# A list scheduler's landing times and its tables, in a kernel of landmark attention, routed experts and a gated unit

## The chip, the cores and the metric

The kernel runs on one core of a Trainium2 chip. The metric is the device time of one execution in microseconds (us). The core has a matrix engine (TensorE, PE in the profile, with PEld for its weight loads), VectorE (DVE), ScalarE (ACT), GpSimd (POOL) and SyncE (SP), which issues DMA transfers. Each engine takes its instructions in the order in which they were written for it; between engines semaphores set the order.

## The reference

```python
def _attn_ref(q, k, v):                  # 4 batches, 8 heads, 576 tokens, 64 wide
    m = 32                               # landmarks: means over 18 tokens each
    q_lm = q.reshape(B, H, m, S // m, D).mean(axis=3)
    k_lm = k.reshape(B, H, m, S // m, D).mean(axis=3)
    A = sm(q, k_lm)                      # sm: scaled scores, softmax by rows
    Bm = sm(q_lm, k_lm)
    C = sm(q_lm, k)
    Z = Bm.T / (norm1(Bm) * norm_inf(Bm) + 1e-06)
    for _ in range(6):
        Z = 2 * Z - Z @ Bm @ Z
    return A @ Z @ C @ v

def _moe_ref(x, w_gate, w1, w2, capacity):   # 2304 tokens, 512 wide, 8 experts
    logits = x @ w_gate
    expert = argmax(logits)              # one expert for each token
    gate = softmax(logits)[expert]
    # the first `capacity` tokens of an expert, in order:
    #   out = gate * (relu(x @ w1[expert]) @ w2[expert]); the others give 0

def reference(...):
    x = attn_out as 2304 x 512           # heads side by side
    x = _moe_ref(x, ...)
    return (sigmoid(x @ w_gate) * (x @ w_val)) @ w_out      # 1536 wide inside
```

All arrays are float32.

## The kernel before

**Blocks.** The 2304 tokens are four batches ("blocks" 0 to 3) of 576. Attention is computed for all four blocks. The experts' work is done per pair of a block and an expert: two such pairs are begun early, under the names "lead" and "1", with the attention of later blocks in between, and a list of the pairs that hold tokens is made once all blocks' routing is known; with these inputs three pairs are active (the third is "2"). The final gated unit follows for each pair. A float32 product on PE is done as products of a high part (`hi`) and a low part (`lo`) of each operand; ACT casts the high part, DVE or POOL subtracts it from the whole to get the low part.

**Stages of a block b.** `load_qk` loads q and k (each as 2 x 2 tiles of 128 x 576). `sums` makes the landmarks, on DVE by one reduction of 128 x 576 per tile, or on POOL, for the (b, q or k) listed in `SUMS`, by five additions for a pair of tiles. `inverse` makes `Bm` (product `pb`) and the six steps of Z: in each, PE makes `pz`, ACT copies it (`rz<-pz`), PE and DVE make the next `rz` from it (`rz<-rz,pz`). A step is thus a chain over three engines, and what PE has between two `pz` covers it. `scores` makes `A` (product `pa`, tile `ea`); `weights` is its softmax: `ma` (maximum, DVE), `ea<-ea,ma` (subtraction, on the engine `SUBS[b]`), exponential (ACT), `ra` (sum and reciprocal, DVE), `ea<-ea,ra` (division, on `NORMS[b]`), transposes into `at` (DVE). `context` makes `C @ v` (`pc`, `pct`, `pv`), `back` folds (`pf`), and routes: `pw`, `pgt`, its copy `lt` on ACT, `pg`, then `dl`, `eq`, `mns` (the chosen expert) on DVE.

**Gate, rows, list.** `gate(b)` takes the exponential `gexp` (ACT), its sum `sgm` and reciprocal (DVE), stores the gates to memory (L1756) and for blocks 0 and 1 loads them back spread over all partitions (`gate_now`, L1760). `parts` and `halves` split `at` of block b into `hi` and `lo`; for blocks 2 and 3 `hi` is a tile `xs` of which there is one only (`xs<-at`, two casts on ACT), so block 3's casts wait until block 2's `xs` has been stored. `lo` is `at<-at,xs`, on the engine `XLO[b]`. `row_store` stores `hi`, `lo` and the fold to memory (L1787, L1787, L1791). `ranks` waits for `mns` of all four blocks: DVE makes `ranks` and `rsum`, PE counts in `pk` and `pr`, and the list follows (`pp`, `prow`, `ptb`). `zero_rows` stores zeros to the output in 18 pieces (L1177).

**Expert weights.** `expert_loads` loads an expert's weights in pieces `w_raw` (L613); a piece of the first matrix is multiplied by a fold (`mm<-w_raw,fold`), one of the second is split into `ws` by ACT's cast and DVE's subtraction. The products with them are `mm<-xa,ws`, `mm<-xb,ws` and `mm<-slot,ws`.

**What sets the order.** All of this is written as streams: Python generators that yield what the next step needs (an engine, slots, events). `Streams.go` takes, among the steps that can begin, the one with the earliest modelled start plus `SLACK` times its urgency (`URGENCY` by stage, `EXTRA` by stage and block), and writes it. `Streams.settle` books the time of what was written: a duration for each operation, and for a DMA a landing time from a rate (`RATE`), after which its event counts as done (`SETTLED` later). So a wrong booking costs nothing by itself; it sets in which place of an engine's in-order queue an operation stands. `HOLD` ties loads and stores to an expert load; `WHOLE` makes `context` wait for all of its tiles; `Streams.fill_up` puts products without use (`idle`) where PE would have little to do. All engines' operations are recorded at one line, L114, by the helper `Clocked`.

Of the kernel before, what the change touches and what calls it, by code (L numbers as in the profile page):

```python
# [23 lines left out]


URGENCY = dict(
    load=200,
    sums=150,
    inverse=0,
    scores=0,  # L30
    context=10,
    back=10,
    weights=30,
    ranks=5,
    number=-20,
    lead_rows=10,
    rows=40,
    lead_loads=-50,
    lead_split=0,
    fold=20,  # L40
    lead=20,
    narrow=40,
)
STEP = 2
AHEAD = 0
SUMS = ()
LOWS = "dve"
XLO = ("pool", "pool", "dve", "dve")
SUBS = ("dve", "dve", "pool", "dve")
NORMS = ("pool", "pool", "pool", "pool")  # L50
SQUARES = ("dve", "dve", "dve", "dve")
HOLD = (15, -1, 3, -1)
EXTRA = dict(back3=-15, context3=-30, inverse3=-60, lead_loads2=-100, lead_loads3=200, lead_rows0=60, lead_rows1=60, lead_split1=30, lead_split2=-60, load3=-30, rows1=60, scores1=-15, sums1=-30, weights2=30)
SLACK = 0.003
SWITCH = (0.09, 0.13)
STICK = 0.02
WHOLE = (1, 0, 1, 1)


def free_size(*aps):  # L60
# [22 lines left out]
def pointers(args):  # L83
    return sum(hasattr(a, "shape") for a in args[2:])


COSTS = {
    "pe": pe_cost,
    "dve": lambda op, args: (0.07 + (0.007 if op == "reciprocal" else 1.04e-3) * free_size(*args)
        + 0.06 * (op == "tensor_scalar" and pointers(args) > 0), 0),  # L90
    "act": lambda op, args: (0.052 + 0.83e-3 * free_size(*args) + 0.09 * (op != "copy" and pointers(args)), 0),
    "pool": lambda op, args: (0.3 + 1.42e-3 * free_size(*args), 0),
}
# [25 lines left out]
class Streams:  # L119
# [8 lines left out]
    LAG = 0.2  # L128
    SHARED = 0.5
    SETTLED = 0.3  # L130
    SAME = 0.13

    WINDOW = 3.4133
    THRESH = 2800
    MARGIN = 1.2
    SOON = 0.0
    SPAN = 3.4
    LANES = 8
    RATE = 0.36
    SHORTEST = 96  # L140

    def __init__(self, nc, slots):
        self.log = []
        for name, engine in zip(COSTS, (nc.tensor, nc.vector, nc.scalar, nc.gpsimd)):
            setattr(self, name, Clocked(name, engine, self.log))
        self.free = dict.fromkeys((*COSTS, "sp"), 2.0)
        self.slots = {kind: [0.0] * n for kind, n in slots.items()}
        self.events = {}
        self.live = []
        self.moving = 0.0  # L150
        self.landed = [0.0] * self.LANES
        self.busy = {}
        self.recent = []
        self.urgency = 0
        self.engine = None
        self.fill = None
# [81 lines left out]
    def settle(self, at, engine):  # L238
        first = True
        for what, name, value, columns in self.log:  # L240
            if what == "run":
                if first:
                    first = False
                elif name != engine:
                    at += self.LAG
                elif name != "pe":
                    at += self.SAME
                at = max(at, self.free[name])
                if name == "pe":

                    warm = self.warm(at)
                    value *= 1 if warm else 2
                    for window in range(int(at / self.WINDOW), int((at + value) / self.WINDOW) + 1):
                        share = min(at + value, (window + 1) * self.WINDOW) - max(at, window * self.WINDOW)
                        self.busy[window] = self.busy.get(window, 0) + columns * share / max(value, 1e-9)
                    self.recent.append((at, columns))
                if name == "pool":

                    self.free["dve"] = max(self.free["dve"], at) + self.SHARED * value
                at += value  # L260
                self.free[name], engine = at, name
            elif what == "move":
                if not first and engine != "sp":
                    at += self.LAG
                first, engine = False, "sp"
                at = max(at, self.free["sp"]) + 0.47
                self.moving = max(at + 1.0, self.moving) + value * 1e-6 / self.RATE
                self.landed = [*self.landed[1:], self.moving + 0.64]
                for event in name:
                    self.events[event] = self.landed[-1] + self.SETTLED  # L270
                self.free["sp"] = max(at, self.landed[0])
            elif what == "free":
                self.slots[name].append(at + self.LAG)
            elif what == "done":
                self.events[name] = at + value + self.LAG
            else:
                self.live.append([(at, engine), value, *self.resume(name, value), name])
        self.log.clear()
        return at, engine
# [43 lines left out]
def tile_attention_moe_glu(  # L323
# [15 lines left out]
    B, S, D = v.shape  # L339
# [116 lines left out]
    lead_rows = (("lead", xa, fold_now, idx_lead), ("1", xb, fold_one, idx_one))  # L456
# [236 lines left out]
    w_raw = {}  # L693
# [79 lines left out]
    works, temps, rows = [], [], []  # L773
# [426 lines left out]
    with actx:  # L1200
# [13 lines left out]
        for t in wrs:  # L1214
# [4 lines left out]
        run = Streams(  # L1219
            nc, dict(bank=7, raw=3, cv=2, qk=6, s3=1, ea=2, ec=2, xs=1, sg=2, w=4, ws0=1, ws1=1, ws2=1, ws3=1)  # L1220
        )
        use(run)
        pe, dve, act, pool = run.pe, run.dve, run.act, run.pool
# [13 lines left out]
        def load_qk(b):  # L1237
            for w, src in enumerate((q, k)):
                for g in range(G):
                    if b < 2:  # L1240
                        t = slot(4 * b + 2 * w + g, F32)
                    else:
                        held = [f"w_raw_lead{HOLD[b]}"] if HOLD[b] >= 0 else []
                        yield "sp", "qk", *held
# [32 lines left out]
        def sums(b, w, g, src):  # L1277
            ld = lds[b % 2]
            free = [f"{what}{b - 2}" for what in ("scores", "context", "inverse")]
            if (b, w) in SUMS:  # L1280
                yield "pool", "s3", *[f"raw{b}{w}{g}{kk}" for kk in range(2)], *free
# [146 lines left out]
        def weights(b, u, ea):  # L1428
# [5 lines left out]
            dve.tensor_reduce(ma, ef, AX.X, ALU.max)  # L1434
            yield (SUBS[b],)
            getattr(run, SUBS[b]).tensor_tensor(ef, ef, ma.unsqueeze(2).broadcast_to(shape), ALU.subtract)
            yield ("act",)
# [7 lines left out]
            dve.reciprocal(ra, ra)  # L1445
            yield (NORMS[b],)
            getattr(run, NORMS[b]).tensor_tensor(ef, ef, ra.unsqueeze(2).broadcast_to(shape), ALU.mult)
            for g in range(G):
# [295 lines left out]
        def gate(b, dl):  # L1744
            yield ("act",)
            ge = wk.tile([P, J, E], F32, tag="gexp", name=f"gexp{b}")
            act.activation(ge, dl, AF.Exp)
            yield ("dve",)
            sg = wk.tile([P, J], F32, tag="sgm", name=f"sgm{b}")
            dve.tensor_reduce(sg, ge, AX.X, ALU.add)  # L1750
            yield ("dve",)
            dve.tensor_scalar_add(sg, sg, 1e-9)
            yield ("dve",)
            dve.reciprocal(gates[:, b], sg)
            yield ("sp",)
            nc.sync.dma_start(gate_dram[b], gates[:, b])  # L1756
            run.moved(4 * S, f"gate{b}")
            if b < LEADS:
                yield "sp", f"gate{b}", *[f"y_lead{d}{half}" for d in range(KD) for half in range(2) if b]
                nc.sync.dma_start(gate_now, gate_dram[b].rearrange("p j -> (p j)").partition_broadcast(128))  # L1760
                run.moved(4 * 128 * S, f"gate_{lead_rows[b][0]}")

        def parts(b, u):

# [6 lines left out]
            act.copy(hi, at[:, :, u])  # L1771
            yield (XLO[b],)
            getattr(run, XLO[b]).tensor_tensor(lo, at[:, :, u], hi.bitcast(F32), ALU.subtract)
            run.done(f"scaled{b}{u}")
# [8 lines left out]
        def row_store(b):  # L1783
            held = [f"w_raw_{lead_rows[b][0]}{HOLD[b]}"] if b < LEADS and HOLD[b] >= 0 else []
            yield "sp", f"scaled{b}0", f"scaled{b}1", f"fold{b}0", f"fold{b}1", *held
            for i, part in enumerate(halves(b)):
                nc.sync.dma_start(  # L1787
                    x_dram[b].rearrange("p (a g u t) -> p a g u t", a=2, g=G, u=2)[:, i], part.bitcast(F32)
                )
                run.moved(4 * 128 * G * T)  # L1790
            nc.sync.dma_start(fold_dram[b].rearrange("p (k m) -> p k m", m=LM), st[b]["fold"])  # L1791
            run.moved(4 * 128 * H // 2 * LM, f"x{b}")
            if b >= LEADS:
                run.release("xs")
            run.done(f"rows{b}")

        def block_list():

# [112 lines left out]
    with tc.For_i(1, n_blocks, 1) as i, tc.manual_schedule(engines=ENGINES):  # L1911
        run = Streams(
            nc, dict(bank=3, sg=2, raw=3, w=4, **{f"ws{k}": 1 for k in range(6)},
                **{f"acc{c}": 1 for c in range(TC)}, **{f"slot{k}": 1 for k in range(4)}, work=10, temp=6)
        )
# [70 lines left out]
```

## Time and profile before

| | us |
|---|---|
| median of 3 runs | 551.8 |
| the runs | 554.17, 550.1, 551.8 |
| profiled execution, its time | 550.84 |
| its span in the profile | 549.1 |
| PE busy | 525.6 |
| mean granted clock of PE, as a share of the full one | 0.99 |

A row of a timeline gives the start and the length of a stretch of one kind of operation, engine, line, operation, output and inputs, shapes and count; in brackets the idle time of its engine before it and what ended that. Where many operations overlap, as on PE, starts and ends of neighbours do too. Times are from the start of the span. The clock column of a stretch is the mean granted clock of PE, where 1.00 is the full one.

### The profile page before, as it was taken

How to read it: one execution, taken by the hardware profiler on the slowest of the kernel's cores; microseconds unless marked ns; L12 is line 12 of the kernel's file. 1: busy time of each engine (PE TensorE's matmuls, PEld its weight loads, DVE VectorE, ACT ScalarE, POOL GpSimd, SP SyncE). 2: the span in 40 equal slices, each digit the busy share in tenths (PEclk: the TensorE clock that was granted, in tenths of full speed). 3: DMA queues.
4: the chain of work that ended last, by engine and by line, in shares of the span. 5: the costliest groups of instructions: out<-in, count | busy, mean ns of one | idle time of the engine just before them, and what ended most of it. 6: DMA issues, size and time to landing. Idle time of an engine off the chain costs nothing. (4 is left out here: it accounts for less than half of the span.)

```text
span 549.1 us, 12467 instructions
## 1 busy us (share of the span) xinstructions
PE 525.6 (96%) x4744; PEld 469.9 (86%) x4744; DVE 443.5 (81%) x1167; ACT 301.7 (55%) x766; POOL 35.6 (6%) x48
## 2 busy tenths in 40 slices
PE   6899999987999999999999999999999999999993
PEld 2457878767999999999999999988799999999882
DVE  7897899967879999989997999954476899987442
ACT  1454525355278777676456766733353577776231
POOL 1112102020000000000010100000300000000003
PEclk9999899999899999999999999999999999999998
DMA  8638971499354555561060000000630000000002
GB/s 297 223 90 273 367 250 47 141 315 286 132 228 157 191 193 190 168 210 50 2 222 2 30 21 1 1 1 0 196 125 1 1 1 2 1 1 1 1 1 91
DMA packets 33187, 61.89 MB, mean 113 GB/s; under 512 B 3584, under 2 KB 13440, under 8 KB 33120
## 3 DMA queue, kind: packets, MB, share of 16 engines
q1 hardware_dynamic: 32016, 57.48, 31.6%
q0 software_dynamic: 1104, 3.54, 1.9%
q8 instruction: 39, 0.64, 0.5%
q14 instruction: 28, 0.23, 0.1%
HBM read 47.76 MB, written 13.25 MB: 111 GB/s over the span
## 5 line engine op out<-in xcount | busy, mean ns | idle before, releaser
L114 PE MATMUL mm<-xa,ws 128*128 128x288 f32 x918 | 134.6, 298 | 1.0 <-ACT sg L114 0.7
L114 PEld LDWEIGHTS mm<-xa,ws 128*128 128x128 f32 x918 | 127.4, 189 | 4.9 <-ACT sg L114 0.9
L114 PE MATMUL acc<-ws,slot 128*128 128x512 f32 x504 | 125.2, 392 | 0.0
L114 PE MATMUL mm<-slot,ws 128*128 128x288 f32 x816 | 116.9, 297 | 0.0
L114 PEld LDWEIGHTS mm<-slot,ws 128*128 128x128 f32 x816 | 111.4, 189 | 1.8 <-issue 0.5
L114 PEld LDWEIGHTS acc<-ws,slot 128*128 128x128 f32 x504 | 91.3, 188 | 16.6 <-issue 0.6
L114 PE MATMUL mm<-xb,ws 128*128 128x288 f32 x636 | 96.5, 297 | 0.0
L114 PEld LDWEIGHTS mm<-xb,ws 128*128 128x128 f32 x636 | 89.4, 189 | 2.9 <-PE pgt L114 0.5
L114 DVE TENSOR_TENSOR work<-mm,work 128x288 f32<-128x288 f32 x66 | 30.0, 454 | 10.8 <-PE mm L114 8.5
L114 ACT CAST slot<-work 128x288 fp32r<-128x288 f32 x56 | 22.0, 431 | 29.0 <-PE acc L114 22.1
L114 DVE TENSOR_TENSOR slot<-work,slot 128x288 fp32r<-128x288 f32 (+2 forms) x80 | 26.6, 363 | 13.4 <-ACT slot L114 13.4
L114 ACT COPY work<-mm 128x288 f32<-128x288 f32 x63 | 24.8, 397 | 18.8 <-PE mm L114 11.5
L114 ACT CAST ws<-wg_res 128x256 fp32r<-128x256 f32 (+1 forms) x60 | 26.8, 448 | 13.3 <-PE mm L114 11.3
L114 DVE TENSOR_TENSOR ws<-wg_res,ws 128x256 fp32r<-128x256 f32 (+1 forms) x60 | 28.3, 473 | 2.9 <-ACT ws L114 2.7
L114 ACT CAST ws<-wv_res 128x256 fp32r<-128x256 f32 (+1 forms) x60 | 26.6, 448 | 5.6 <-PE mm L114 4.1
L114 ACT CAST ws<-rows 128x256 fp32r<-128x256 f32 x66 | 26.7, 405 | 5.4 <-DVE rows L114 3.1
L114 DVE TENSOR_TENSOR ws<-wv_res,ws 128x256 fp32r<-128x256 f32 (+1 forms) x60 | 28.2, 473 | 1.0 <-ACT ws L114 0.8
L114 DVE TENSOR_TENSOR ws<-rows,ws 128x256 fp32r<-128x256 f32 x66 | 27.6, 418 | 0.8 <-ACT ws L114 0.8
L114 DVE TENSOR_TENSOR ws<-wo_res,ws 128x512 fp32r<-128x512 f32 x36 | 24.5, 689 | 1.4 <-ACT ws L114 1.0
L114 ACT CAST ws<-wo_res 128x512 fp32r<-128x512 f32 x36 | 21.8, 619 | 6.4 <-DVE wo_res L114 3.5
L114 ACT ACTIVATE slot<-mm 128x288 fp32r<-128x288 f32 x40 | 16.2, 410 | 12.9 <-PE mm L114 12.6
L114 DVE SCALAR_TENSOR_TENSOR slot<-mm,slot 128x288 fp32r<-128x288 f32 x40 | 17.9, 447 | 3.9 <-ACT slot L114 3.6
(243 smaller groups left out, 701.8 us busy)
## 6 DMA issues: line engine op xcount, KB each, us to landing
w_raw<-in_moe_w SPq DMA_DIRECT2D x48, 256.0 KB, 4.1
raw_g<-in_moe_w_gate SPq DMA_DIRECT2D x12, 512.0 KB, 3.8
raw_v<-in_moe_w_val SPq DMA_DIRECT2D x12, 512.0 KB, 3.5
raw_o<-in_moe_w_out SPq DMA_DIRECT2D x12, 512.0 KB, 3.8
out<-zeros SPq DMA_DIRECT2D x18, 256.0 KB, 4.7
vs<-in_v SPq DMA_DIRECT2D x8, 512.0 KB, 5.1
slot<-in_q SPq DMA_DIRECT2D x8, 288.0 KB, 5.8
slot<-in_k SPq DMA_DIRECT2D x8, 288.0 KB, 6.1
```

Of the source, the lines that this page charges most:

```text
L114: return getattr(self.engine, op)(*args, **kwargs)
```

## The change

Two kinds of edit. The bookings: the store of the gates counts as done at a fixed time behind its issue, the load that spreads it is booked at more than twice its size, events of `w_raw` come 1.0 instead of 0.3 behind the modelled landing, the rate of the transfers is 0.39 instead of 0.36, and the tile `xs` is free for block 3 when block 2's row store has landed, no more when it was issued. The tables: urgencies, holds and the engines of four kinds of operation. The stage `sums` of block 3 goes to POOL (`SUMS`), `lo` of blocks 2 and 3 goes from DVE to POOL (`XLO`), the subtraction of blocks 0, 1 and 3 from DVE to POOL (`SUBS`), the division of blocks 0 and 1 from POOL to DVE (`NORMS`). Lines of the changed file stand 1 to 3 below those of before.

```diff
 URGENCY = dict(
-    load=200,
+    load=40,
     sums=150,
     inverse=0,
     scores=0,
-    context=10,
-    back=10,
-    weights=30,
-    ranks=5,
+    context=20,
+    back=0,
+    weights=10,
+    ranks=-200,
     number=-20,
-    lead_rows=10,
-    rows=40,
-    lead_loads=-50,
-    lead_split=0,
-    fold=20,
+    lead_rows=60,
+    rows=10,
+    lead_loads=-100,
+    lead_split=30,
+    fold=10,
     lead=20,
-    narrow=40,
+    narrow=60,
 )
...
-SUMS = ()
+SUMS = ((3, 0), (3, 1),)
...
-XLO = ("pool", "pool", "dve", "dve")
-SUBS = ("dve", "dve", "pool", "dve")
-NORMS = ("pool", "pool", "pool", "pool")
+XLO = ("pool", "pool", "pool", "pool")
+SUBS = ("pool", "pool", "pool", "pool")
+NORMS = ("dve", "dve", "pool", "pool")
 SQUARES = ("dve", "dve", "dve", "dve")
-HOLD = (15, -1, 3, -1)
-EXTRA = dict(back3=-15, context3=-30, inverse3=-60, lead_loads2=-100, lead_loads3=200, lead_rows0=60, lead_rows1=60, lead_split1=30, lead_split2=-60, load3=-30, rows1=60, scores1=-15, sums1=-30, weights2=30)
+HOLD = (11, 3, 11, 15)
+EXTRA = dict(context3=-30, inverse1=-15, inverse3=-60, lead_loads1=100, lead_loads3=-60, lead_rows0=60, lead_rows3=100, load0=100, load1=100, rows0=60, sums0=30, sums1=-60, sums2=-60, weights2=30)
...
-WHOLE = (1, 0, 1, 1)
+WHOLE = (0, 0, 1, 1)
...
     SETTLED = 0.3
+    LATE = 1.0
...
-    SOON = 0.0
+    SOON = 0.6
...
-    RATE = 0.36
+    RATE = 0.39
...
-        self.free = dict.fromkeys((*COSTS, "sp"), 2.0)
+        self.free = dict.fromkeys((*COSTS, "sp"), 2.0) | {"sp": 0.75}
...
                 for event in name:
-                    self.events[event] = self.landed[-1] + self.SETTLED
+                    self.events[event] = self.landed[-1] + (self.LATE if "w_raw" in event else self.SETTLED)
...
             nc.sync.dma_start(gate_dram[b], gates[:, b])
-            run.moved(4 * S, f"gate{b}")
+            run.moved(4 * S)
+            run.done(f"gate{b}", 4.0)
             if b < LEADS:
                 yield "sp", f"gate{b}", *[f"y_lead{d}{half}" for d in range(KD) for half in range(2) if b]
                 nc.sync.dma_start(gate_now, gate_dram[b].rearrange("p j -> (p j)").partition_broadcast(128))
-                run.moved(4 * 128 * S, f"gate_{lead_rows[b][0]}")
+                run.moved(9 * 128 * S, f"gate_{lead_rows[b][0]}")
...
             run.moved(4 * 128 * H // 2 * LM, f"x{b}")
+            run.done(f"rows{b}")
             if b >= LEADS:
+                yield None, f"x{b}"
                 run.release("xs")
-            run.done(f"rows{b}")
```

The order that comes out differs on every engine from the start of the program. Three places show it. Numbers behind a name tell apart tiles of one name; they are drawn anew in each kernel.

DVE at the steps of block 1's inverse, before (`rz` are the steps' results, `ws_69<-w_raw` the split of an expert weight, `slot` a unit's activations, `at` the transposes of block 1):

```order
L114 TENSOR_TENSOR rz_988<-rz_962,pz_979 128x2x32
L114 SCALAR_TENSOR_TENSOR slot_866<-mm,slot_866 128x288
L114 STREAM_TRANSPOSE at_564<-ea_606 128x288
L114 SCALAR_TENSOR_TENSOR slot_991<-mm,slot_991 128x288
L114 TENSOR_TENSOR ws_69<-w_raw,ws_69 128x512
L114 TENSOR_TENSOR rz_1029<-rz_988,pz_1020 128x2x32
```

and after:

```order
L114 TENSOR_TENSOR rz_942<-rz_906,pz_933 128x2x32
L114 TENSOR_TENSOR ws_72<-mm,ws_72 128x512
L114 TENSOR_TENSOR rz_967<-rz_942,pz_958 128x2x32
L114 STREAM_TRANSPOSE at_633<-ea_660 128x288
L114 SCALAR_TENSOR_TENSOR slot_814<-mm,slot_814 128x288
L114 SCALAR_TENSOR_TENSOR slot_850<-mm,slot_850 128x288
L114 TENSOR_TENSOR rz_990<-rz_967,pz_981 128x64
```

The split of the weight that was just loaded (`ws_69<-w_raw`) stood ahead of the last `rz` but one and now comes behind the last, five operations later; ACT's cast for it moved in the same way, behind the last copy `rz<-pz`.

SP ahead of block 2's row store, before (`out<-zeros` are the zero stores, `gate_rows<-gates` the store of block 2's gates):

```order
L1177 DMA out<-zeros 128x4x128 x8
L1756 DMA gate_rows<-gates 96x6
L1177 DMA out<-zeros 128x4x128 x2
L613 ISA
L613 DMA w_raw<-in_moe_w 128x512
L1177 DMA out<-zeros 128x4x128 x2
L1787 DMA x_rows<-xs_2189 128x1152
```

and after (`vs` is block 3's v):

```order
L1267 DMA vs_1809<-in_v 64x512
L1178 DMA out<-zeros 128x4x128 x17
L614 ISA
L614 DMA w_raw<-in_moe_w 128x512
L614 ISA
L614 DMA w_raw<-in_moe_w 128x512
L1178 DMA out<-zeros 128x4x128
L1789 DMA x_rows<-xs_2172 128x1152
```

Seventeen of the zero stores now stand in one row right behind the load of block 3's v, and only two weight loads and one zero store stand between them and block 2's row store; the gates' stores of blocks 2 and 3 come behind it.

POOL from the division of block 2 on, before:

```order
L114 TENSOR_TENSOR ea_1333<-ea_1333,ra_1591 128x576
L114 TENSOR_TENSOR ea_1371<-ea_1371,ra_1615 128x576
L114 MEMSET ranks 96x960
L114 TENSOR_TENSOR ea_1723<-ea_1723,ra_2112 128x576
L114 TENSOR_TENSOR ea_1739<-ea_1739,ra_2149 128x576
```

and after, from the last of the four groups of sums on (`s` is the sums' own tile, `ld` the landmarks, all of block 3):

```order
L114 TENSOR_TENSOR s_1606<-qk_1367 128x384
L114 TENSOR_TENSOR s_1606<-s_1606,qk_1367 128x384
L114 TENSOR_TENSOR s_1606<-s_1606 128x2x96
L114 TENSOR_TENSOR ld_160<-s_1606 128x64
L114 TENSOR_TENSOR ld_160<-ld_160,s_1606 128x64
L114 TENSOR_TENSOR ea_1313<-ea_1313,ra_1685 128x576
L114 TENSOR_TENSOR ea_1328<-ea_1328,ra_1709 128x576
L114 TENSOR_TENSOR ea_1990<-ea_1990,ma_2095 128x576
L114 TENSOR_TENSOR ea_2017<-ea_2017,ma_2098 128x576
L114 MEMSET ranks 96x960
L114 TENSOR_TENSOR at_1312<-at_1312,xs_2172 128x2x288 x2
```

The divisions of block 2 now stand behind the landmarks of block 3, and the subtractions of block 3 and the low parts of block 2 (`at<-at,xs`) are new on POOL.

## Rows read from the trace of the kernel before

**Rows 1.** The page, its first part: busy time of each engine.

```profile
PE 525.6 (96%) x4744; PEld 469.9 (86%) x4744; DVE 443.5 (81%) x1167; ACT 301.7 (55%) x766; POOL 35.6 (6%) x48
```

**Rows 2.** Waits of PE, 42.75 to 150 us: in total, times, longest.

```profile
PE pk L114 <- DVE rsum L114: 2.8, 1, 2.8
...
PE pz L114 <- issue: 0.6, 1, 0.6
```

**Rows 3.** Timeline of PE, 137 to 147 us.

```profile
137.15 0.60 PE L114 MATMUL pk<-ones,rsum 96*32 96x1 f32 x14 [2.79 <-DVE rsum L114]
...
138.42 1.79 PE L114 MATMUL mm<-xb,ws 128*128 128x288 f32 x6
...
140.33 1.70 PE L114 MATMUL mm<-slot,ws 128*128 128x288 f32 x6
```

**Rows 4.** Timeline of PE, 55 to 67 us.

```profile
56.12 0.33 PE L114 MATMUL pz<-rz 32*32 32x32 f32 x16 [1.57 <-DVE rz L114]
56.37 3.22 PE L114 MATMUL mm<-xa,ws 128*128 128x288 f32 x12
...
64.50 1.86 PE L114 MATMUL mm<-xa,ws 128*128 128x288 f32 x12
```

**Rows 5.** Windows: length, PE, PEld, DVE, ACT, POOL busy, clock, DMA share, GB/s.

```profile
56.10:60.00 3.90, 3.88 (x44) 3.54 (x44) 2.24 (x6) 1.80 (x5) 1.42 (x1) 0.56 1.05 367
75.00:95.00 20.00, 19.34 (x280) 16.08 (x265) 19.09 (x53) 8.43 (x28) 4.91 (x4) 1.00 0.37 113
...
137.15:147.10 9.95, 9.95 (x80) 9.34 (x81) 8.76 (x28) 1.96 (x4) 0.00 (x0) 0.83 0.29 97
```

**Rows 6.** Timeline of DVE, 134 to 138 us.

```profile
135.41 0.20 DVE L114 TENSOR_REDUCE sgm<-gexp 96x6 f32<-96x48 f32 x1 [3.02 <-ACT gexp L114]
```

**Rows 7.** Timeline of ACT, 129 to 136 us.

```profile
133.99 1.25 ACT L114 CAST xs<-at 128x576 fp32r<-128x576 f32 x2 [2.90 <-DMA x_rows<-xs]
```

**Rows 8.** Timeline of SP, 108 to 132 us: issue of transfers.

```profile
118.28 6.55 SPq L1177 DMA_DIRECT2D out<-zeros  x8
...
129.21 0.64 SPq L1787 DMA_DIRECT2D x_rows<-xs  x1
```

**Rows 9.** Timeline of ACT, 54 to 57 us.

```profile
54.59 0.62 ACT L114 CAST ws<-w_raw 128x512 fp32r<-128x512 f32 x1 [1.73 <-DMA w_raw<-in_moe_w]
...
55.41 0.20 ACT L114 COPY rz<-pz 128x64 f32<-128x64 f32 x1
```

**Rows 10.** Timeline of PE, 22 to 27 us: steps of block 0's inverse.

```profile
22.47 0.47 PE L114 MATMUL pz<-rz 32*32 32x64 f32 x16 [0.69 <-DVE rz L114]
...
26.05 0.43 PE L114 MATMUL pz<-rz 32*32 32x64 f32 x16 [0.59 <-DVE rz L114]
```

**Rows 11.** Timeline of PE, 96 to 137 us: the products `pgt` of blocks 2, 3.

```profile
119.26 0.68 PE L114 MATMUL pgt<-at,wr 128*32 128x288 f32 x3 [1.04 <-issue]
...
128.97 0.69 PE L114 MATMUL pgt<-at,wr 128*32 128x288 f32 x8
```

**Rows 12.** Groups of DVE by form, 9 to 150 us: busy, mean ns of one.

```profile
L114 DVE TENSOR_REDUCE ld<-qk 128x32 f32<-128x576 f32 x16 | 11.2, 734 | 0.0
...
L114 DVE TENSOR_TENSOR ea<-ea,ma 128x576 f32<-128x576 f32 x6 | 4.5, 753 | 0.1
```

**Rows 13.** Groups of POOL by form, whole span.

```profile
L114 POOL TENSOR_TENSOR ea<-ea,ra 128x576 f32<-128x576 f32 x8 | 9.1, 1158 | 43.3 <-DVE rz L114 35.6 <-DVE ra L114 5.8 <-ACT ws L114 1.9
...
L114 POOL TENSOR_TENSOR xa<-at,xa 128x576 fp32r<-128x576 f32 x2 | 2.8, 1405 | 2.7 <-ACT xa L114 2.7
L114 POOL TENSOR_TENSOR ea<-ea,ma 128x576 f32<-128x576 f32 x2 | 2.6, 1312 | 25.4 <-DVE ma L114 25.4
```

**Rows 14.** Timelines of POOL and DVE, 80 to 94 us.

```profile
85.88 1.16 POOL L114 TENSOR_TENSOR ea<-ea,ma 128x576 f32<-128x576 f32 x1 [3.41 <-DVE ma L114]
...
86.40 1.19 DVE L114 TENSOR_TENSOR ws<-w_raw,ws 128x512 fp32r<-128x512 f32 x1
...
88.63 0.69 DVE L114 TENSOR_TENSOR ws<-w_raw,ws 128x512 fp32r<-128x512 f32 x1
```

## The prediction

> **What bounds the kernel now.** The page's first part comes first: PE is busy for 96% of the span and POOL for 6% [rows 1], so time can come only from PE's gaps, from stretches at the lower clock, and from work taken off PE. The order gives PE 4910 instructions in both kernels, and from its 2356th on the same order, so units "1" and "2" and the tail should take what they take now. What is left is the stretch up to about 150 us, and I read PE's waits in it.
>
> The largest wait is 2.8 us, of `pk` for `rsum` [rows 2]. [...] The chain back: DVE's `sgm` waited 3.02 for ACT's `gexp` [rows 6]; `gexp` stood in ACT's queue behind block 3's two `xs` casts, which waited 2.90 for the landing of block 2's row store [rows 7]; SP had issued that store only at 129.21, behind zero stores, eight of which held it for 6.55 [rows 8]. ACT is in order, so one late landing held the gate and with it the block list.
>
> The second place is the last step of block 1's inverse: `pz` at 56.12 waited 1.57, and the 12 `mm` behind it took 3.22 against 1.86 [rows 4] at a clock of 0.56 [rows 5]. There ACT's cast of an expert weight waited 1.73 for its DMA, with the copy that the step needs behind it [rows 9].
>
> The rest is small: 0.6 and 1.0 with releaser "issue" [rows 2, 11], and in block 0's inverse 0.69 before the first step and 0.59 before a later one [rows 10].
>
> **The change part by part.** The sum goes against the profiled execution, 550.84 (span 549.1 and 1.74 around it).
>
> *Landing of the row store, earlier store.* In the changed order 17 zero stores go in one burst, long ahead, and block 2's store has behind it only two weight loads and one zero store to pass. SP's stretch for the 17 is 17 x 0.82 = 14 us [rows 8]; those loads wait behind it, and nothing shown to PE so far does, since the weights there are for later products. Let T be the start of block 2's `pgt`. Its casts stand close behind the copy of that product: 0.7 + 0.4 + 1.25 + some 0.8 for two short operations between them, so the store is issued by about T + 3.7, and at 4.8 from issue to release (129.21 to 133.99 [rows 7, 8]) it has landed at T + 8.5. Block 3's casts are wanted behind its own `pgt`, which now comes 9.7 after block 2's [rows 11]; the order has 12 `mm` fewer (-1.9) and 32 fold products more (+1.1) between them, and with product and copy this is T + 10. So the casts no longer wait, 1.5 to spare; and 36 `mm` instead of 24 lie ahead of `pk`. That takes 2.8, and with it the lower clock: 1.79 + 1.70 - 1.86 = 1.6. **-4.4**, between -4.4 and 0. What is late next there is DVE's `rsum`, some small operations behind `gexp`; the 12 extra `mm` (1.9) cover them.
>
> *Late expert weights.* ACT and DVE now have the last copy and addition of block 1's inverse ahead of the cast, so a late DMA holds only work that PE wants later: 1.57 + (3.22 - 1.86) = **-2.9**, between -2.9 and 0. Next behind it is the weight itself; before its products stand others, so I book nothing.
>
> *Subtractions of blocks 0, 1 and 3 to POOL, divisions of 0 and 1 to DVE.* A subtraction takes 0.75 on DVE [rows 12] and 1.31 on POOL [rows 13]. In block 0's head two leave DVE's row ahead of `rz`, where PE waited 0.69 [rows 10], and two divisions come back later, between steps. Gain up to 2 x 0.75 = 1.5; loss, where POOL's longer run is waited for, up to 2 x 0.56 = 1.1. Part of the 0.69 is the nearest row: **-0.5**.
>
> *The sums of block 3, and POOL's other work.* POOL gains 20 operations for sums, 6 subtractions and 4 of `lo`, and loses 4 divisions. The sums have no row: by elements against 1158 ns for 576 [rows 13], the five of a group take 0.77 + 0.77 + 0.39 + 0.13 + 0.13 = 2.2, 8.8 for four; at a full operation each, 20 x 1.16 = 23.2. I take 12, nearer to the lower end because the pieces are short. With 6 x 1.31 + 4 x 1.41 - 4 x 1.16 = 8.9 that is 21 us more on POOL. DVE is relieved of 8 reductions at 0.73, and of 4 `lo` and 6 subtractions, and given 4 divisions, all these at the subtraction's 0.75 for the same elements [rows 12]: 5.9 + 3.0 + 4.5 - 3.0 = 10.4. PE waited little for DVE where these stand (20.00 long, 19.34 busy from 75 to 95 [rows 5]), so the relief alone is worth 0 to -0.9.
>
> Against it stands the neighbour: DVE's `ws` took 1.19 while POOL's subtraction ran and 0.69 two us later without it [rows 14]. At 0.5 for each 1.16 of POOL, 21 us could stretch DVE by 9, about what it was relieved of. On PE's path lie only stretched operations ahead of a step of an inverse: 12 steps and DVE operations in blocks 2 and 3 at 0.5 are the upper end, 6; three of them are my value: **+1.5**, between -0.9 and +6.
>
> [...]
>
> *Thinner cover of block 3's inverse.* In the new order five of its steps have only `pct`, `pf` or 8 `pa` between them instead of 6 `mm`. A step with nothing behind it cost PE 0.59 [rows 10]. Five give 3.0, none 0; I take two: **+1.2**.
>
> *Moved without a price.* Idle fillers (14 in both), holds and loads: their work stands in stretches where PE has products in front. The "issue" waits (1.6) fell where zeros were stored; the burst is stored elsewhere, so they may go or come: 0, from -1.6 to +1.6.
>
> Sum: -4.4 - 2.9 - 0.5 + 1.5 + 1.2 = -5.1, so 545.7. The median of the runs shown, 551.8, lies 0.96 above the profiled execution; half of it added gives **546.2**.
>
> **The rivals.**
>
> *Everything is covered* and the small waits go too: no contention on PE's path and no thin steps (-2.7), the issue waits gone (-1.6), is 546.2 - 4.3 = 541.9, with 540.5 to 544 around it. For it: DVE has slack there [rows 5]. Against: short covers showed waits already [rows 10].
>
> *A wait takes the place of the one removed.* Block 3's inverse or the list waits once for 1.5 to 2.8 at another place and the clock falls behind it as it did twice: 546.2 + 2.8 + 1.6 = 550.6, 548.5 to 551.5. For it: both waits of over 1.5 brought the lower clock with them [rows 4, 5].
>
> *The change does not do what it says*: block 3's casts still wait for the landing, as with the burst of zeros still under way at T or a store that lands later than 4.8 behind loads. Then only the second place is gained: 550 to 551.
>
> *Slower: POOL's queue becomes the bound.* POOL is in order, and block 2's divisions are on it behind sums of block 3. At 23.2 for these in place of 12 the last landmark comes 11.2 later and `pb` of block 3 stands still for what of it is not covered. From 5.6 uncovered on the kernel is slower than before; half uncovered gives 551.8, all with one fall of the clock 546.2 + 11.2 + 1.6 = 559, and with the contention of the longer queue (another 3 of its 6) 562. I write 552 to 562. For it: POOL's three kinds of full operation take 1.2 to 1.4 each [rows 13]. Against it: the pieces have two thirds, a third and a ninth of such a one's elements, and POOL is idle for 94% now [rows 1].
>
> **How the numbers follow.** Forecast 0.45, with 544 to 548.5 as its own range; everything covered 0.23; a wait in place of another 0.20; the change not doing what it says 0.03; POOL's queue 0.09. Within 1% of 551.8, about what a measurement of this kernel can tell from no change, is 546.3 to 557.3. Half of the forecast's case and all of the covered one are faster: 0.22 + 0.23 = 0.45. The other half, the two middle cases and the lower half of POOL's are same: 0.23 + 0.20 + 0.03 + 0.04 = 0.50. Slower is POOL's upper half, 0.05. The range runs from 541.5, which leaves out a third of the covered case, to 551.5, which leaves out POOL's: about 0.83.
>
> **What would show it.** In the profile of the changed kernel: no wait of `pk` over 0.5 us and a clock near 1.00 behind it; block 3's first `xs` cast without a DMA as releaser; block 1's last step with under 0.5 of wait; POOL's sums near 12 us in all, and DVE's two-input operations at 1.0 to 1.2 beside them; block 3's `pz` with waits of 0.2 to 0.6. I am wrong if PE's waits before 150 us are as long in sum as now but named by POOL or by `pb`, if the clock falls at a new place, or if the stretch behind 150 us takes another time.

## The result, and the profile after

| | before | after |
|---|---|---|
| median, us (4 runs each) | 550.95 | 543.57 |
| lowest to highest | 549.92 to 554.17 | 542.87 to 545.19 |
| profiled execution, its time | 550.84 | 544.08 |
| its span | 549.1 | 542.2 |

The ratio is 0.986 (95% interval 0.981 to 0.991): 1.4% faster. The forecast was 546.2 (range 541.5 to 551.5).

The page's first part of the changed kernel, against [rows 1]:

```profile
PE 521.8 (96%) x4744; PEld 466.8 (86%) x4744; DVE 443.7 (82%) x1153; ACT 302.7 (56%) x766; POOL 59.0 (11%) x74
```

PE is busy 3.8 us less with the same instructions; the two stretches at the lower clock [rows 4, 5], which are gone, make about 2.5 of it. POOL is busy 23.4 more (21 was forecast). DVE, which by the forecast's count was relieved of 10.4 us of work, is busy for as long as before (443.7 against 443.5): its other operations grew by about as much. PE's waits of the changed kernel from 42 to 150 us and from there on (in total, times, longest):

```profile
PE mm L114 <- DVE slot L114: 0.8, 1, 0.8
PE pn L114 <- DVE bb L114: 0.5, 1, 0.5
PE pk L114 <- DVE rsum L114: 0.4, 1, 0.4
PE pz L114 <- DVE rz L114: 0.2, 1, 0.2
PE pp L114 <- DVE act_b L114: 0.2, 1, 0.2
...
PE mm L114 <- ACT sg L114: 2.4, 1, 2.4
PE acc L114 <- DMA w_raw<-in_moe_w: 1.4, 1, 1.4
```

Against [rows 2]: `pk` waits 0.4 in place of 2.8, no "issue" wait is left, and what else PE waits for are four small waits on DVE, those for `slot` and `bb` new. The last two lines stand behind 150 us. The timeline of PE in the changed kernel, 10 to 150 us, against [rows 3, 4, 11]:

```profile
50.95 0.33 PE L114 MATMUL pz<-rz 32*32 32x32 f32 x16
51.20 5.85 PE L114 MATMUL mm<-xa,ws 128*128 128x288 f32 x42
...
110.52 0.69 PE L114 MATMUL pgt<-at,wr 128*32 128x288 f32 x8
...
120.60 1.07 PE L114 MATMUL mm<-xb,ws 128*128 128x288 f32 x6 [0.78 <-DVE slot L114]
121.59 0.69 PE L114 MATMUL pgt<-at,wr 128*32 128x288 f32 x8
...
128.97 0.58 PE L114 MATMUL pk<-ones,rsum 96*32 96x1 f32 x14 [0.38 <-DVE rsum L114]
...
137.15 0.90 PE L114 MATMUL ptb<-spots,shift 96*128 96x160 f32 x6
```

`pk` comes 8.2 earlier than before (137.15), and `ptb`, the last product of the list, which stood at 146.38, 9.2 earlier. Of these 9.2 the end of the kernel kept 6.9: the wait for `sg` is 2.4 where it was 0.7, and an `acc` waits 1.4 for a weight.

SP and ACT of the changed kernel (timelines, 90 to 130 and 108 to 130 us), against [rows 7, 8]:

```profile
95.40 17.11 SPq L1178 DMA_DIRECT2D out<-zeros  x17
...
114.89 0.44 SPq L1789 DMA_DIRECT2D x_rows<-xs  x1
```

```profile
122.43 0.40 ACT L114 COPY lt<-pgt 128x288 f32<-128x288 f32 x1 [0.32 <-PE pgt L114]
122.73 1.25 ACT L114 CAST xs<-at 128x576 fp32r<-128x576 f32 x2
```

With T = 110.52 the store is issued at T + 4.4 (forecast 3.7), and block 3's casts begin at T + 12.2 (forecast 10) without a wait.

POOL's sums (groups by form: busy, mean ns), against [rows 13]:

```profile
L114 POOL TENSOR_TENSOR s<-s,qk 128x384 f32<-128x384 f32 x4 | 4.7, 1178 | 0.2
L114 POOL TENSOR_TENSOR s<-qk 128x384 f32<-128x384 f32 x4 | 3.5, 866 | 21.1 <-DMA qk<-in_q 20.9
...
L114 POOL TENSOR_TENSOR s<-s 128x192 f32<-128x192 f32 x4 | 3.4, 844 | 0.2
...
L114 POOL TENSOR_TENSOR ld<-ld,s 128x64 f32<-128x64 f32 x4 | 1.7, 420 | 0.3
L114 POOL TENSOR_TENSOR ld<-s 128x64 f32<-128x64 f32 x4 | 1.6, 398 | 0.3
```

They take 14.9, between the bounds of 8.8 and 23.2 and above the 12 taken: the shorter operations took more than their share of the elements (0.40 at 64, 0.87 at 384). What the prediction did not have is on DVE (timelines of DVE, 60 to 130 us, and POOL, 60 to 125 us, of the changed kernel):

```profile
95.67 0.92 DVE L114 TENSOR_SCALAR rb<-rb 128x2 f32<-128x2 f32 x1
...
114.29 1.41 DVE L114 TENSOR_SCALAR eq<-dl 96x48 f32<-96x48 f32 x1
...
116.09 1.04 DVE L114 TENSOR_SCALAR sgm<-sgm 96x6 f32<-96x6 f32 x1
...
125.41 1.41 DVE L114 TENSOR_SCALAR eq<-dl 96x48 f32<-96x48 f32 x1
```

```profile
95.40 1.16 POOL L114 TENSOR_TENSOR ea<-ea,ra 128x576 f32<-128x576 f32 x1 [0.53 <-ACT eb L114]
...
112.84 2.81 POOL L114 TENSOR_TENSOR at<-at,xs 128x576 fp32r<-128x576 f32 x2 [1.05 <-ACT xs L114]
115.95 1.16 POOL L114 TENSOR_TENSOR ea<-ea,ra 128x576 f32<-128x576 f32 x1 [0.29 <-DVE eq L114]
...
123.48 3.30 POOL L114 TENSOR_TENSOR at<-at,xs 128x576 fp32r<-128x576 f32 x2 [3.98 <-ACT xs L114]
```

The two `eq`, of 96 x 48, end at 115.70 and 126.82, the POOL operations at 115.65 and 126.78; `sgm` ends at 117.13, POOL's at 117.11. Each stood until POOL was through. So did `rb` of block 3's inverse: it ends at 96.59, POOL's division at 96.56, where the same operation of block 2 took 0.17. `rb` makes `bb`, for which `pn` then waits 0.50.

### The profile page after: what moved, and what is told of

Its sections match the earlier page's. It is cut to its first block, busy times and chain, and to the rows that moved or that the text cites. A ratio compares the mean times of both kernels' runs of the same rounds, so it can differ in the third digit from the quotient of the medians.

```text
span 542.2 us, 12480 instructions
## 1 busy us (share of the span) xinstructions
PE 521.8 (96%) x4744; PEld 466.8 (86%) x4744; DVE 443.7 (82%) x1153; ACT 302.7 (56%) x766; POOL 59.0 (11%) x74
## 5 line engine op out<-in xcount | busy, mean ns | idle before, releaser
L114 PE MATMUL mm<-xa,ws 128*128 128x288 f32 x918 | 132.9, 296 | 2.7 <-ACT sg L114 2.4
L114 PEld LDWEIGHTS mm<-xa,ws 128*128 128x128 f32 x918 | 126.0, 188 | 6.6 <-ACT sg L114 2.6
L114 DVE TENSOR_TENSOR work<-mm,work 128x288 f32<-128x288 f32 x66 | 29.8, 452 | 11.9 <-PE mm L114 10.2
L1156 POOL DMA_INDIRECT out<-rows,idx_lead x5 | 5.4, 1079 | 178.4 <-DVE rows L114 157.5
```

What stands on the lines that cost most here:

```text
L114: return getattr(self.engine, op)(*args, **kwargs)
L1156: scatter = nc.gpsimd.indirect_dma_start(out[:, :], bass.IndirectOffsetOnAxis(ap=idx[0:n, c : c + 1], axis=0), o[0:n], None, bounds_check= ...
```

## The experiments

Every ratio is to the kernel before, run on the same chip, with its 95% interval.

**1. One booking alone, in the kernel before** (e1, and once more as e9).

```diff
+            run.done(f"rows{b}")
             if b >= LEADS:
+                yield None, f"x{b}"
                 run.release("xs")
-            run.done(f"rows{b}")
```

> The kernel before, with one booking of the change alone: the tile xs is free for block 3 when block 2's row store has landed. On ACT block 3's two xs casts move behind gexp and some activations; PE, DVE, POOL and SP keep their order. Theory 1 (the late landing held gexp, and with it rsum and pk): pk's wait of 2.8 falls under 0.5 and the clock behind it stays at 1.00; the profiled time falls by 2.8 to 4.4 from that of before, to about 547. Rival (the wait is only moved: the casts now hold the weight cast and the activations behind them): pk no longer waits, but an mm behind it waits 1.5 to 3 for ws or slot, and the time is within 1 us of before.

545.73 against 551.27: 0.9878 (0.982 to 0.994).

> The kernel before with the booking of the row store's landing alone, once more, to narrow its interval (0.982 to 0.994 so far). Theory 1 (the wait of pk and the clock behind it are the main part of the gain): ratio 0.988 to 0.992. Rival (the first four runs fell low by chance, the wait alone is worth under 3 us): 0.995 to 1.0. In the profile pk without a wait over 0.5, a clock of 1.00 behind it, and issue waits of another size than last time.

544.96 against 550.95: 0.9884 (0.985 to 0.992). Timelines of PE in e1, and in e9:

```profile
42.24 0.27 PE L114 MATMUL mm<-w_raw,fold_now 64*32 64x128 f32 x1 [1.40 <-issue]
...
56.28 0.33 PE L114 MATMUL pz<-rz 32*32 32x32 f32 x16
...
127.81 0.69 PE L114 MATMUL pgt<-at,wr 128*32 128x288 f32 x8
...
133.14 0.60 PE L114 MATMUL pk<-ones,rsum 96*32 96x1 f32 x14
...
141.02 0.90 PE L114 MATMUL ptb<-spots,shift 96*128 96x160 f32 x6
```

```profile
54.74 0.33 PE L114 MATMUL pz<-rz 32*32 32x32 f32 x16 [1.06 <-DVE rz L114]
...
126.59 0.69 PE L114 MATMUL pgt<-at,wr 128*32 128x288 f32 x8
...
131.92 0.60 PE L114 MATMUL pk<-ones,rsum 96*32 96x1 f32 x14
...
139.81 0.90 PE L114 MATMUL ptb<-spots,shift 96*128 96x160 f32 x6
```

`pk` does not wait, and from it to `ptb` it takes 7.9 in both, where before took 9.23. The mechanism of theory 1 holds, the rival falls: no `mm` behind it waits, and the clock from `pk` to `ptb` is 1.00 in both. The size does not hold in e1: the profiled time fell by 5.3, where 2.8 to 4.4 was expected; the ratio of e9 is as expected. By the medians the booking alone gives 5.5 to 6.0 us. In the profiles its own part stands between block 3's `pgt`, up to which nothing differs in the order, and `ptb`: 17.4 before (128.97 [rows 11] to 146.38), 13.2 in both here, so 4.2; the rest of the fall lies ahead of it. There block 1's last `pz` waited 1.57 before [rows 4], here 0 and 1.06, with the same order up to there. That wait belongs to the execution.

**2. The late weight alone, in the kernel before** (e2).

```diff
-                    self.events[event] = self.landed[-1] + self.SETTLED
+                    self.events[event] = self.landed[-1] + (2.0 if event == "w_raw_lead8" else self.SETTLED)
```

> The kernel before, with the first split weight of the lead expert alone booked 2.0 late instead of 0.3. On ACT and DVE its cast and subtraction move behind the last but one copy and addition of block 1's inverse; PE keeps its order. Theory 1 (a late weight stood ahead of the step): the wait of 1.57 of block 1's last pz goes, the 12 mm behind it take 1.9 instead of 3.2, and the time falls by 2 to 3 us, to about 548. Rival (the weight itself is wanted soon behind): an mm waits 1 to 2 for ws, and the clock falls there; within 1 us of before.

550.93 against 551.27: 0.9988 (0.996 to 1.001). The timeline of PE in e2:

```profile
42.49 0.27 PE L114 MATMUL mm<-w_raw,fold_now 64*32 64x128 f32 x1 [1.40 <-issue]
...
56.62 0.33 PE L114 MATMUL pz<-rz 32*32 32x32 f32 x16
...
128.90 0.69 PE L114 MATMUL pgt<-at,wr 128*32 128x288 f32 x8
...
137.14 0.91 PE L114 MATMUL pk<-ones,rsum 96*32 96x1 f32 x14 [2.84 <-DVE rsum L114]
...
149.03 0.89 PE L114 MATMUL ptb<-spots,shift 96*128 96x160 f32 x6
```

The step's wait is gone, as it was in e1 without this edit, and nothing is gained: neither theory's time nor the rival's new wait. The `pk` wait stands again at 2.84, and the clock behind it was worse: windows of e2, with the clock as the third number from the end:

```profile
137.14:149.90 12.76, 12.76 (x81) 11.98 (x82) 8.90 (x28) 1.97 (x4) 0.00 (x0) 0.62 0.27 88
```

From `pk` to `ptb` 11.9 against 7.9 without the wait: this time the lower clock cost 4.0, in the profile before 1.35 [rows 5]. This is the slowest of e2's ten executions, and the one with the lowest clock (0.982).

**3. Low parts on DVE, in the changed kernel** (e3, and again as e12). POOL's booking stays, so that no other order moves.

```diff
-            getattr(run, XLO[b]).tensor_tensor(lo, at[:, :, u], hi.bitcast(F32), ALU.subtract)
+            if b >= LEADS:
+                pool.book("tensor_tensor", (lo, at[:, :, u], hi), {})
+                nc.vector.tensor_tensor(lo, at[:, :, u], hi.bitcast(F32), ALU.subtract)
+            else:
+                getattr(run, XLO[b]).tensor_tensor(lo, at[:, :, u], hi.bitcast(F32), ALU.subtract)
```

> The changed kernel with lo of blocks 2 and 3 issued on DVE at the places of the order where POOL has them; all bookings and every other order stay. Theory 2 (a short TENSOR_SCALAR on DVE stands until the POOL operation beside it ends: eq<-dl took 1.41 twice, ending within 0.1 us of POOL's at<-at,xs): both eq take about 0.2, the mm wait of 0.78 for slot at 120.6 and pk's wait of 0.38 go, and the time is up to 1 us below that of the changed kernel. Rival (eq is slow by itself or by its inputs): eq stays at 1.4. Second rival (DVE's order is full): eq is short, but four more lo of 0.78 and their wait for ACT's casts hold DVE, PE waits 1 to 3 more around 113 to 127.

542.00: 0.9809 (0.976 to 0.986). DVE and POOL in e3:

```profile
117.71 0.18 DVE L114 TENSOR_SCALAR eq<-dl 96x48 f32<-96x48 f32 x1
...
118.28 1.11 DVE L114 TENSOR_SCALAR sgm<-sgm 96x6 f32<-96x6 f32 x1
...
128.33 0.18 DVE L114 TENSOR_SCALAR eq<-dl 96x48 f32<-96x48 f32 x1
```

```profile
118.20 1.16 POOL L114 TENSOR_TENSOR ea<-ea,ra 128x576 f32<-128x576 f32 x1 [4.50 <-DVE eq L114]
```

Without the POOL operation beside them both `eq` take 0.18; `sgm`, still beside one, stands until its end (119.39 against 119.36). Theory 2 holds for `eq`. The waits of 0.78 and of `pk` are gone, and from block 2's `pgt` to `pk` it takes 17.2 (113.59 to 130.77) against 18.4.

> The changed kernel with lo of blocks 2 and 3 on DVE, once more. From its profile (block 2's pgt to pk in 17.2 us against 18.4) it should be 0.5 to 1.3 below the changed kernel: ratio to before 0.980 to 0.985 where the changed kernel had 0.986. If it is 0.985 to 0.989, what the two waits gave is lost behind them, or is within what executions differ by.

541.59: 0.9825 (0.979 to 0.986), as expected, the stretch 17.5; PE waits 0.3 for `slot` again. The medians of e3 and e12 lie 0.9 to 2.0 us below the two of the changed kernel (543.57 above, 542.86 in e7), but the intervals overlap, and e8 below, with the same edit, has 543.13: perhaps a better kernel, not shown.

**4. The sigmoid ahead of a conversion** (e4): `narrow=60` becomes `narrow=100`.

> The changed kernel with the urgency of narrow at 100 instead of 60 (a higher number comes later). Up to the list nothing moves; on ACT the table load and the first sigmoid come ahead of the first half of a raw_o, where the changed kernel has them behind it and behind its DMA. Theory 3 (the 2.41 that PE waits for sg at 165.9 is ACT's wait for that DMA and its operation, which before did not show because PE was 9 us later): the wait for sg falls to 0.6 to 1.4 and the time by 1 to 1.8, to about 542. Rival (the sigmoid is bound by the table load and the split weight ahead of it): it stays at 2 or more. Second rival (the conversion then comes late): PE waits later for a ws by as much as was won.

543.33: 0.9835 (0.979 to 0.988). The wait for `sg` was 1.25 in place of 2.41. But the changed kernel itself shows 1.05 in a second profile (e7), so this says nothing of theory 3.

**5. Sums of block 3 on DVE** (e5), as reductions at the place of POOL's first addition, in the changed kernel with its bookings.

```diff
-                pool.tensor_tensor(s3, dc[..., 0], dc[..., 1], ALU.add)
+                pool.book("tensor_tensor", (dc[..., 0],), {})
+                for kk in range(2):
+                    dv = src[:, kk].rearrange("p (c m r) -> p m c r", c=J, r=SEGP)
+                    nc.vector.tensor_reduce(ld[:, w, 2 * g + kk], dv, AX.XY, ALU.add)
...
```

> The changed kernel with the sums of block 3 as DVE's reductions, at the places of the order where POOL has the first of the five additions; bookings and every other order stay. Theory 2 (POOL work beside DVE costs DVE as much as it takes off it): eight reductions of 0.74 come back (5.9 on DVE), xa<-yt falls from 0.67 to about 0.5 and rn and rb from 0.50 and 0.35 to about 0.2 where the sums stood, so the time is within 2 us of the changed kernel, and pn's wait of 0.50 goes. Rival (the relief of DVE is what the change gains from 60 to 100): PE waits 2 to 5 more for DVE between 75 and 97 and the time is 546 to 549.

544.73: 0.9900 (0.986 to 0.994), on the chip where the changed kernel had 542.86 and 0.9862. PE waits of e5 (timeline, 42 to 548 us):

```profile
79.31 0.46 PE L114 MATMUL pn<-bb,mask 128*128 128x128 f32 x2 [1.20 <-DVE bb L114]
87.07 0.43 PE L114 MATMUL pz<-rz 32*32 32x64 f32 x16 [0.90 <-DVE rz L114]
```

1.9 above the changed kernel, just inside theory 2's 2 and below the rival's time. The intervals overlap, but each of the five executions (544.5 to 545.7) took longer than each of the six of the changed kernel on this chip (541.9 to 544.1, e7). From 75 to 97 us PE waits 2.3 for DVE, where the changed kernel has no wait of over 0.2 up to the 0.50 of `pn`, as the rival says: DVE's relief outweighs what POOL costs it, by less than the rival has it. `pn` of block 3 still waits, for 0.26, and that of block 2 waits now. `xa<-yt` fell to 0.55 as expected, but `rn` (0.51) and `rb` (0.35) did not: the subtractions stand beside `rn`, and with them on DVE (e6) it takes 0.16.

**6. Subtractions and divisions as before** (e6), at the places of the changed order.

```diff
-            getattr(run, SUBS[b]).tensor_tensor(ef, ef, ma.unsqueeze(2).broadcast_to(shape), ALU.subtract)
+            pool.book("tensor_tensor", (ef,), {})
+            (nc.gpsimd if b == 2 else nc.vector).tensor_tensor(ef, ef, ma.unsqueeze(2).broadcast_to(shape), ALU.subtract)
...
-            getattr(run, NORMS[b]).tensor_tensor(ef, ef, ra.unsqueeze(2).broadcast_to(shape), ALU.mult)
+            getattr(run, NORMS[b]).book("tensor_tensor", (ef,), {})
+            nc.gpsimd.tensor_tensor(ef, ef, ra.unsqueeze(2).broadcast_to(shape), ALU.mult)
```

> The changed kernel with the subtractions of blocks 0, 1 and 3 on DVE and the divisions of blocks 0 and 1 on POOL, as before, at the same places of the order. Theory 1 (the step of block 0 was sized at -0.5): block 0's last pz comes 0.3 to 1.5 later than in the changed kernel, the first mm<-xa 0.3 to 1, and the time is up to 1 us above it. Rival (POOL's subtraction is waited for by the exponential, so DVE is better): it is 0.5 to 1 below.

543.68: 0.9867 (0.983 to 0.991), 0.8 above the changed kernel: theory 1's sign and size, within what executions differ by. Block 0's last `pz` comes 1.0 later than in e7 (27.90 against 26.86), as expected; the first `mm<-xa` 1.8 later (43.30 against 41.54), which is more.

**7. The changed kernel again** (e7).

> The changed kernel once more, for comparison on the same chip. If the w_raw wait of 1.41 at 386.8 and the waits with releaser issue are a matter of the execution and not of the order, the wait at 386.8 is absent or of another size, and issue waits of 0.3 to 1.5 stand at other places; the waits on DVE (pn 0.50, mm 0.78, pk 0.38) and for sg (2.4) stand again within 0.1. If they belong to the order, all stand again.

542.86: 0.9862 (0.983 to 0.990). Timeline of PE in e7:

```profile
97.68 0.46 PE L114 MATMUL pn<-bb,mask 128*128 128x128 f32 x2 [0.50 <-DVE bb L114]
...
120.82 1.06 PE L114 MATMUL mm<-xb,ws 128*128 128x288 f32 x6 [0.72 <-DVE slot L114]
129.19 0.57 PE L114 MATMUL pk<-ones,rsum 96*32 96x1 f32 x14 [0.38 <-DVE rsum L114]
...
164.79 1.88 PE L114 MATMUL mm<-xa,ws 128*128 128x288 f32 x12 [1.05 <-ACT sg L114]
```

These three waits on DVE stand again to 0.06. The one on a DMA does not, 0.49 of `acc` for 1.41, nor does that for `sg`, 1.05 for 2.41, which names ACT, but ACT had a DMA to wait for ahead of it (0.92 for `raw_o` at 163.50 in the first profile).

**8. Low parts on DVE and narrow at 100 together** (e8).

> The changed kernel with lo of blocks 2 and 3 on DVE and narrow at 100, both edits that took a wait away when made alone. If they add up: no wait of mm for slot or of pk, sg's wait at 1.0 to 1.6, and the time 1.5 to 3 us below that of the changed kernel, some 541. If the second only gives the first's gain back (the conversion of the last unit's weights is what bounds sg), the wait for sg is over 2 and the time equals that of the run with lo on DVE.

543.13: 0.9864 (0.983 to 0.990). The waits are as expected (none for `slot` or of `pk`, 1.49 for `sg`), the time is not: the two do not add up, and nothing beats the changed kernel by more than the intervals.

**9. Bookings without tables, tables without bookings** (e10, e11).

> All bookings and constants of the change (landing of the row store, LATE, the gates' store and load, SOON, RATE, SP's start) with the tables of before. Every engine's order is drawn anew. If the bookings are what gains, 543 to 546, with no wait of pk over 0.5. If the tables do (they were fitted to other bookings, so these lose their fit), 549 to 556, with waits at places that neither kernel has.

543.08: 0.9848 (0.982 to 0.988), and `pk` does not wait: as expected if the bookings are what gains.

> The tables of the change with all bookings and constants of before. Every engine's order is drawn anew: block 2's row store comes long ahead of block 3's casts, which stand ahead of gexp as before. If tables alone gain: 543 to 546, pk without a wait over 0.5. If a table is worth only what fits its bookings: 549 to 556, with a wait of over 1 us at a new place, which the profile names.

551.02: 0.9997 (0.996 to 1.003). The bookings alone give the whole gain, with the tables of before and without one operation more on POOL; the tables alone give none. Each of the two is a single order, drawn anew: this says what these two programs take, and not which of the other bookings adds to the landing's 5.5 to 6.0. Timelines of PE and SP in e11:

```profile
33.55 0.44 PE L114 MATMUL pz<-rz 32*32 32x32 f32 x16
...
113.42 0.25 PE L114 MATMUL py<-bb 32*32 32x32 f32 x3 [2.34 <-issue]
```

```profile
118.71 0.73 SPq L1788 DMA_DIRECT2D x_rows<-xs  x1
```

There `pk` waits only 0.4, though the booking of the landing is the old one: the tables put block 2's row store 4.4 behind its `pgt`, as in the changed kernel. But block 0's last `pz` comes at 33.55 (28.41 before), with PE at a mean clock of 0.88 up to 42 us, and `py` waits 2.3 with releaser "issue". One wait went and others came.

## Why the prediction held, point by point

**Landing of the row store, -4.4.** The mechanism is right and the largest part, but the size was low by the medians: alone it gives 5.5 to 6.0 (e1, e9; by the intervals 3.6 to 9.9 and 4.4 to 8.4). The step that was mis-sized is the clock, 1.6: that is what the 12 `mm` behind `pk` [rows 3] took beyond 12 at the full clock [rows 4], with a granted clock of 0.83 there [rows 5], and behind the same wait it cost 1.35 in one execution and 4.0 in another (e2, at 0.62), so 2.8 + 1.35 to 4.0 = 4.2 to 6.8. The clocks of all executions bear this out. In 41 of the kernel before, the mean granted clock was 0.982 to 0.994, 0.987 on the mean; in ten of the changed kernel it was 0.994 to 0.998, 0.996 on the mean. Among the 41, a clock lower by 0.01 goes with 3 to 6 us more. By that, an estimate, the difference of 0.009 stands for 3 to 5 of the 7.4 us, the waits that go with it included.

The cause in the changed kernel needs care. Taking the booking `yield None, f"x{b}"` out of it leaves every engine's order the same, and block 3's casts stand ahead of `gexp` there as before. So there it is the store's earlier place on SP that removes the wait, and e11 has the same without the booking; in the kernel before and in e10 the casts move behind `gexp`. The terms that the prediction names for the store add up to T + 3.15, not T + 3.7; measured was T + 4.4, and there was room, because the casts came 2.2 later than forecast.

**Late weights, -2.9: wrong.** Made alone, the edit gains 0.3 (the interval runs from a loss of 0.8 to a gain of 2.1). I took a wait that goes back to a DMA in one profile for a property of the order. With the order of before it was 1.57, 0 and 1.06 in three executions, and in e1 and e2, where it was absent, an "issue" wait of 1.40 stood at 42 us, with a clock of 0.79 from 42 to 50 us.

**Block 0's head, -0.5.** The first `mm<-xa` comes at 42.17 instead of 42.75; e6 gives 0.8, within what executions differ by: the same `mm` stands at 41.54 in e7.

**POOL and DVE, +1.5.** The waits that came are 0.78, 0.38 and the 0.50 of `pn`, 1.66 in all, so the size is right, but the price per operation is wrong, and that the sum came out is luck. I priced each DVE neighbour at 0.5; in fact the short TENSOR_SCALARs shown above stood until POOL's operation ended, up to 1.2 longer (`eq` 1.41 against 0.18 in e3). DVE's relief, which I put at 0 to -0.9, is worth about 1.9 in the sums alone, what POOL costs DVE already taken off (e5). The row that I read as slack of DVE [rows 5] has it busy for 19.09 of 20.00 us. In the four cases shown, the ends of the two operations lie 0.02 to 0.05 us apart, and with both `eq` at 0.18 (e3) `pk` does not wait.

**Thinner cover, +1.2.** Measured 0.23, in the one `pz` of block 3 that has only `pf` (0.43 us) ahead of it; with 16 `pa` (0.72) or four `pct` (0.66) there is no wait. So the mechanism is right, but two thin steps at 0.59 were too many and too dear.

**The issue waits, 0.** They took 1.9 before and nothing in the two profiles of the changed kernel; in its variants e3, e4 and e8 they are back with 1.3, 1.2 and 0.5. Their sizes change with the execution. In the kernel before, the DMA share is 1.02 and 0.96 in the 4 us ahead of the two over 0.4 (0.60 and 1.04), but in e2 it is 0.6 to 0.7 in the 3 us ahead of the one of 1.40, so what makes them is open.

**Behind 150 us the same: wrong in the profile.** The waits for `sg` and for one weight are 3.2 longer there, of which 2.3 reach the end, and 0.9 longer in e7. The prediction had named this as a sign of being wrong. PE arrives 9 us earlier at weights that are converted at their own pace; that this bounds `sg` was argued, not shown (e4).

**The sum.** To `ptb`: -2.4 and -1.05 for `pk` and the clock, -2.9 block 1's step, -1.9 issue waits, -0.85 four small waits, -0.6 head, +1.5 new waits (0.78, 0.50, 0.23) is -8.2 of 9.2; 1.0 has no name. These are two executions, and -2.9 of it goes back to a wait that was 0 and 1.06 in two others of the same order; the issue waits differ between executions too. That the forecast of -5.1 came as near the median's -7.4 as it did is in part luck: one term was too low (the landing), one too high (the weight), and the relief was taken at nothing. With the 0.3 that e2 measured for the weight the same sum is -2.5.

## What to carry to other kernels

In this list scheduler booked landing times were worth more than new tables: one event moved to where the trace has it gave 1.2% in the kernel before, all bookings 1.5%, and the new tables without them nothing. Before a term rests on a wait, follow its chain to the start and take a second profile. The waits for DVE's own work that e7 repeats came out alike to 0.06 us; a wait with releaser "issue", or one whose chain goes back to a DMA, did not, even where the profile names DVE (block 1's `pz`: 1.57, 0, 1.06) or ACT (`sg`: 2.41, 1.05). The wait of `pk` of 2.8 us cost its own length and then 1.35 (before) and 4.0 (e2) in clock.

## What the runs showed of the hardware

A DVE TENSOR_SCALAR on 96 x 48 or 96 x 6 elements took 0.14 to 0.18 us alone and 1.0 to 1.4 beside a POOL TENSOR_TENSOR, ending with it (0.02 to 0.05 apart); one on 128 x 2 took 0.92 against 0.17. POOL's additions cost 0.40 us at 128 x 64 and 0.84 to 1.18 at 128 x 192 and 128 x 384. Behind a wait of 2.8 us PE's granted clock was 0.83 in one execution and 0.62 in another over the next 10 to 13 us; what decides between them stays open, as does what ends the "issue" waits.
